# Attention scores cut into column tiles for the later tokens only, with two head pairs run last token first

## The chip, the cores and the metric

The kernel runs on one core of one Trainium2 chip. The metric is the device time of one execution in microseconds (us). The kernel before takes 520.03 us, the median of three runs (518.87 to 521.28).

## The reference

A linear attention with a decaying state feeds a two-layer network. For each of 4 batches and 8 heads (head size 48), over 768 tokens:

```
cur = einsum('bhd,bhe->bhde', u[None] * kt, vt)
y[:, :, t] = einsum('bhd,bhde->bhe', rt, state + cur)
state = wt[:, :, :, None] * state + einsum('bhd,bhe->bhde', kt, vt)
```

Then, with `x` the 3072 x 384 matrix of all heads' `y`: `h = x @ w_in` (2048 columns), `g = h` where `h > 0` and `exp(h) - 1` elsewhere, and the result is `g @ w_out` (384 columns).

## The kernel before, in words

The tokens are cut into 6 blocks of 128. A *unit* is one block of one batch: 24 units, numbered block by block, so units 8 to 23 are the third to the sixth block. In a unit the 8 heads are 4 *pairs* p; the two heads of a pair, q = 0 and 1, lie on partitions 0 to 47 and 64 to 111.

The work of a unit, with the short names that the order tables use:

- `es`, `gs` (DVE): running products of the decay; `kh` (DVE, line 404) multiplies k by them, `rh` (line 401) multiplies r.
- `s` (PE, line 458): the scores. For each pair and head one product of k (48 x 128 sources) with r (48 x 128 tokens), into two PSUM tiles `pa`, one for q = 0 and one for q = 1, each 128 sources x (4 pairs x 128 tokens). That is 8 products per unit in 32-bit floats; the trace has two matmul records for each such product (16 per unit).
- `sp` (ACT or POOL): writes the two tiles `am` with the diagonal term and zeros; `mk` (DVE, line 461, two per unit) copies into `am` the scores of later tokens (token after source), by the 0/1 mask `upper`.
- `v` (PE, line 488): y, in four column tiles of 32 output rows: from block 1 on 12 products of the state `st` with r, and always 16 products of v with `am`.
- `t` (PE, 466) transposes k, `kt` (ACT) copies it out, `u` (PE, 505) multiplies it with v, `up` (DVE, 513) adds that to the state; `sc` (DVE, 473) decays the state; `xh` (ACT) and `xl` (DVE, 498) split y into two parts for the network.

The network works on a block of all four batches (512 columns), in 16 slices of 128 hidden rows: `g1` (PE, line 248, nine matmuls), `r1`, `r2` (ACT), `stt` (DVE, 259), `gh` (ACT), `gl` (DVE, 270), `g2` (PE, line 281, nine matmuls). Blocks 0 and 1 run some slices in halves of 256 columns, so that there are 108 slices. The scores of the blocks ahead are worked off between the slices.

What sets the order: a table `ORDER` written out by hand gives each engine its list of tasks, and an engine works through its list in that order, waiting where an input or a buffer is not there. `ph`, the result of `g1`, has two buffers, so a `g1` waits for the `stt` of two slices before. The PSUM tiles `pa` are three, shared by `s`, `v`, `t`, `u` in turn. On PE the table reads, at the places that matter here, `t.8 s.9 v.8 g1.39 g2.36 g1.40 g2.37 u.8 v.9 s.10 g1.41`, and on DVE `mk.9.0 xl.8 up.8 rh.10 gl.38 stt.39 kh.11 mk.10.0 mk.10.1`. The table is the same in both kernels.

Of the kernel before, what the change touches and what calls it, by code (L numbers as in the profile page):

```python
# [8 lines left out]
F32 = mybir.dt.float32  # L9
F32R = mybir.dt.float32r  # L10
BF16 = mybir.dt.bfloat16
U32 = mybir.dt.uint32
# [4 lines left out]
ALU = mybir.AluOpType  # L17
AX = mybir.AxisListType

B, H, S, D = 4, 8, 768, 48  # L20
DM, DFF = 384, 2048
P = 128
C = 128
NC = S // C
NP = H // 2
# [5 lines left out]
CW = C + 1  # L31
# [1 line left out]
WKR = dict(w=(0, W1), k=(W1, W1 + K1), r=(W1 + K1, W1 + K1 + R1))  # L33
NU = NC * B
FH = (6, 6)
SIGN = "DVE"
WARM = 10


def _pieces():  # L40
# [274 lines left out]
def rwkv_elu_kernel(ctx, tc, wkr, rk, vp, u, uz, gkrw, gv, gu, w_in, w_out, out):  # L315
    nc = tc.nc
# [7 lines left out]
    cst = pool("cst", 1)  # L324
# [7 lines left out]
    tt, stt, act = nc.vector.tensor_tensor, nc.vector.scalar_tensor_tensor, nc.scalar.activation  # L332
# [6 lines left out]
    reset = cst.tile([R2, 2, NP, CW], F32, name="reset")  # L339
    lim = cst.tile([R2, 1], F32, name="lim")  # L340
    ident = cst.tile([P, P], F32, name="ident")
    upper = cst.tile([P, C], F32, name="upper")
    upper4 = upper.bitcast(U32).unsqueeze(1).broadcast_to([P, 4, C])
    ub = cst.tile([P, DM], F32, name="ub")
    ubd = cst.tile([R2, NP, 2], F32, name="ubd")
    tops = [cst.tile([P, 2, NK, P], U32, name=f"wt{n}") for n in range(SLOTS["wt"])]
# [4 lines left out]
    def constants():  # L351
        nc.scalar.preload_act_table_set("natural_log_exp_and_others")
        nc.vector.memset(reset, 2.0 ** -62)
        nc.vector.memset(reset[:, 0, :, C:CW], 1.0)
        nc.vector.memset(lim, -(2.0 ** 60))
        make_identity(nc, ident)
        nc.vector.memset(upper, 1.0)
        nc.gpsimd.affine_select(out=upper, in_=upper, pattern=[[1, C]], compare_op=ALU.is_gt,
                                fill=0.0, base=0, channel_multiplier=-1)
        for t in tops:  # L360
            nc.gpsimd.memset(t, 0)
        nc.gpsimd.memset(st, 0.0)
        nc.vector.memset(ones_c, 1.0)

    def warm():
        for _ in range(WARM):
            nc.tensor.matmul(first["accs"]()[0][:, 0:P], ident, ident, start=True, stop=True)
# [33 lines left out]
        tt(u_["r"], u_["r"], u_["eg"][:, 1, :, 0:C], ALU.mult)  # L401

    def k_hat(u_):
        tt(u_["k"], u_["k"], u_["eg"][:, 0, :, 1:CW], ALU.mult)

    def flag(u_):
        junk = at.tile([R2, 2 * NP * CW], BF16, tag="junk", name="junk", bufs=1)
# [43 lines left out]
    def score(u_):  # L451
        u_["pa"] = pa = [ps_a.tile([P, NP, C], F32, tag="pa", name="pa_s") for q in range(2)]
        for _ in range(FILL.get(("s", u_["i"]), 0) * (u_["i"] > 1)):
            nc.tensor.matmul(pa[0][:, 0], ident, ident, start=True, stop=True)
        for p in range(NP):
            for q in range(2):
                rs = slice(64 * q, 64 * q + D)
                nc.tensor.matmul(pa[q][:, p], u_["k"][rs, p, :], u_["r"][rs, p, :], start=True, stop=True)  # L458

    def mask(u_, q):  # L460
        nc.vector.copy_predicated(u_["am"][q], upper4, u_["pa"][q])  # L461

    def trans(u_):
        u_["pt"] = pt = ps_a.tile([P, NP, R2], F32, tag="pa", name="pa_t")
# [10 lines left out]
    def value(u_):  # L475
        c, b, v, am, rp = (u_[n] for n in ("c", "b", "v", "am", "r"))
        u_["py"] = py = ps_a.tile([P, NK, C], F32, tag="pa", name="pa_y")
        jobs = []
        if c > 0:
            for n in range(3 * NP):  # L480
                p, i = divmod(n, 3)
                jobs.append((n, st[:, b, p, 32 * i:32 * i + 32], rp[:, p, :]))
        for p, x in ROUNDS:
            jobs.append((3 * p + (0, 1, 1, 2)[x], v[:, P * p + 32 * x:P * p + 32 * x + 32], am[x // 2][:, p, :]))
        for n, (blk, l, r) in enumerate(jobs):
            k, j = divmod(blk, 4)
            same = [m for m, y in enumerate(jobs) if y[0] % 4 == j]
            nc.tensor.matmul(py[32 * j:32 * j + 32, k], l, r, start=(n == same[0]), stop=(n == same[-1]))  # L488
# [77 lines left out]
    for c in range(NC):  # L566
        fh = FH[c] if c < len(FH) else 0
        steps.append([(f, 0, N // 2) for f in range(fh)] + [(f, N // 2, N) for f in range(fh)] + [(f, 0, N) for f in range(fh, NF)])

    add(("const",), "POOL", constants)  # L570
    add(("warm",), "PE", warm, [("const",), ("es", 0)])
    add(("ubd",), "SP", lambda: load_u(True))
    add(("ub",), "SP", lambda: load_u(False))
    for u_ in units:
        i, c, b = u_["i"], u_["c"], u_["b"]
# [5 lines left out]
        add(("gs", i), "DVE", lambda u_=u_: g_scan(u_), [("es", i)])  # L581
        add(("rh", i), "DVE", lambda u_=u_: r_hat(u_), [("gs", i), ("ld_r", i)])
        add(("kh", i), "DVE", lambda u_=u_: k_hat(u_), [("es", i), ("ld_k", i)])
        if 0 < c:
            add(("pc", i), "ACT", lambda u_=u_: decay(u_), [("es", i)])
# [7 lines left out]
        else:  # L593
            e = DIAG[i]
# [6 lines left out]
        else:  # L601
            add(("sp", i), "POOL", lambda u_=u_: spread(u_), [("md", i)])
        add(("s", i), "PE", lambda u_=u_: score(u_), [("rh", i), ("kh", i), ("sp", i)])
        for q in range(2):
            add(("mk", i, q), "DVE", lambda u_=u_, q=q: mask(u_, q), [("s", i), ("sp", i)])
# [7 lines left out]
        if b:  # L613
            after.append(("v", i - 1))
        add(("v", i), "PE", lambda u_=u_: value(u_), after)
        add(("xh", i), "ACT", lambda u_=u_: x_high(u_), [("v", i)])
        add(("xl", i), "DVE", lambda u_=u_: x_low(u_), [("xh", i)])
# [11 lines left out]
    for c in range(NC):  # L629
        fns = mlp(nc, w_h, w_l, ps_acc, ps_h, ml, home, stg, out[:, c * N:(c + 1) * N], last=c == NC - 1)  # L630
        for f, lo, hi in steps[c]:
            s, n = dict(f=f, lo=lo, hi=hi), len(seq)
# [22 lines left out]
    for u_ in units:  # L655
        i, c = u_["i"], u_["c"]
# [13 lines left out]
    for f in range(NF):  # L670
        p = "raw0" if f % 3 == 0 or f == NF - 1 else "x1a" if f % 3 == 1 else "x1b"
# [10 lines left out]
    with tc.manual_schedule():  # L682
        for t in plan.order():
            k = t["key"]
# [128 lines left out]
```

## Time and profile before

| | |
|---|---|
| median of 3 runs | 520.03 us (518.87 to 521.28) |
| the profiled execution's own time | 521.82 us |
| its span, first to last instruction | 520.1 us |
| PE busy | 502.2 us (97%), 4065 matmul records |
| DVE / ACT / POOL busy | 331.2 / 276.1 / 66.0 us |
| mean granted TensorE clock | 0.995 |
| score matmuls (line 458) | 384 records in 24 units |

A row of a group reads: line, engine, operation, output and inputs, shapes, count, then busy time in us, the mean duration of one in ns, and the engine's idle time before them with what ended it. A row of the timeline reads: start, time from the first start to the last end, engine, line, operation, names, shapes, count. Matmuls overlap, so the count times the mean is far above the busy time; the end of a matmul record is modelled, and where it matters the starts are used: from the time of a timeline row one record's own duration is taken off, which leaves first start to last start.

### The profile page before, as it was taken

How to read it: one execution, taken by the hardware profiler on the slowest of the kernel's cores; microseconds unless marked ns; L12 is line 12 of the kernel's file. 1: busy time of each engine (PE TensorE's matmuls, PEld its weight loads, DVE VectorE, ACT ScalarE, POOL GpSimd, SP SyncE). 2: the span in 40 equal slices, each digit the busy share in tenths (PEclk: the TensorE clock that was granted, in tenths of full speed). 3: DMA queues.
4: the chain of work that ended last, by engine and by line, in shares of the span. 5: the costliest groups of instructions: out<-in, count | busy, mean ns of one | idle time of the engine just before them, and what ended most of it. 6: DMA issues, size and time to landing. Idle time of an engine off the chain costs nothing.

```text
span 520.1 us, 10015 instructions
## 1 busy us (share of the span) xinstructions
PE 502.2 (97%) x4065; PEld 423.7 (81%) x4065; DVE 331.2 (64%) x533; ACT 276.1 (53%) x558; POOL 66.0 (13%) x74
## 2 busy tenths in 40 slices
PE   4999999999999999999999999999999999999994
PEld 4788988889988888788888888888888788878884
DVE  7998889967677765756757476647474744333332
ACT  4979798757554434635444445325744524544441
POOL 2000000002131130701203021020220210000000
PEclk9989999999999999999999999999999999999999
DMA  7969463322224231322121336001440100000001
GB/s 223 325 218 281 140 204 113 92 68 88 78 77 134 86 100 39 124 87 88 56 70 38 94 105 194 2 1 38 143 127 8 69 1 1 26 36 3 0 2 64
DMA packets 26596, 47.35 MB, mean 91 GB/s; under 512 B 2736, under 2 KB 9008, under 8 KB 26544
## 3 DMA queue, kind: packets, MB, share of 16 engines
q1 hardware_dynamic: 26112, 45.86, 28.6%
q8 instruction: 34, 0.56, 0.4%
q10 hardware_dynamic: 432, 0.79, 0.4%
q14 instruction: 18, 0.15, 0.1%
HBM read 41.92 MB, written 4.72 MB: 90 GB/s over the span
## 4 chain that ended last, share of the span: by engine, by line
PE 86%; DVE 5%; ACT 2%; issue 1%; DMA 1%; SPq 0%; DVEq 0%; ACTq 0%
PE ph L248 36%; PE acc L281 36%; PE pa_y L488 6%; PE pa_s L458 4%; PE pa_u L505 2%; PE pa_t L466 1%; DVE m L259 1%; DMA r<-in_wkr_dram 1%; PE pa_d L428 1%; DVE gl L270 1%; DVE am L461 1%; ACT gh L266 0%; DVE r L401 0%; ACT m L256 0%; DVE xl L498 0%
## 5 line engine op out<-in xcount | busy, mean ns | idle before, releaser
L248 PE MATMUL ph<-xh,w_h 128*128 128x512 f32 (+1 forms) x324 | 122.1, 377 | 1.1 <-DVE m L259 1.0
L253 ACT ACTIVATE m<-ph 128x512 f32<-128x512 f32 (+1 forms) x108 | 59.3, 549 | 118.6 <-PE ph L248 78.6
L281 PE MATMUL acc<-gh,w_h 128*128 128x512 f32 (+1 forms) x325 | 120.7, 371 | 0.0
L248 PE MATMUL ph<-xl,w_h 128*128 128x512 f32 (+1 forms) x324 | 119.4, 369 | 1.2 <-DVE xl L498 1.2
L259 DVE SCALAR_TENSOR_TENSOR m<-m,ph 128x512 f32<-128x512 f32 (+1 forms) x108 | 67.0, 624 | 82.5 <-ACT m L256 82.2
L248 PE MATMUL ph<-xh,w_l 128*128 128x512 f32 (+1 forms) x324 | 119.5, 369 | 0.0
L281 PE MATMUL acc<-gl,w_h 128*128 128x512 f32 (+1 forms) x325 | 119.0, 366 | 0.3 <-DVE gl L270 0.3
L281 PE MATMUL acc<-gh,w_l 128*128 128x512 f32 (+1 forms) x325 | 118.7, 365 | 0.0
L270 DVE TENSOR_TENSOR gl<-m,gh 128x512 fp32r<-128x512 f32 (+1 forms) x108 | 68.9, 641 | 52.0 <-ACT gh L266 48.2
L266 ACT CAST gh<-m 128x512 fp32r<-128x512 f32 (+1 forms) x108 | 61.6, 571 | 70.3 <-PE acc L281 41.6
L248 PEld LDWEIGHTS ph<-xh,w_h 128*128 128x128 f32 x324 | 61.7, 191 | 13.3 <-DVE m L259 2.8
L248 PEld LDWEIGHTS ph<-xl,w_h 128*128 128x128 f32 x324 | 61.8, 191 | 10.5 <-DVE xl L498 1.4
L248 PEld LDWEIGHTS ph<-xh,w_l 128*128 128x128 f32 x324 | 61.8, 191 | 10.4 <-DVE w_l L552 0.2
L281 PEld LDWEIGHTS acc<-gl,w_h 128*128 128x128 f32 x325 | 61.3, 189 | 10.9 <-DVE gl L270 1.3
L281 PEld LDWEIGHTS acc<-gh,w_h 128*128 128x128 f32 x325 | 61.2, 188 | 10.8 <-issue 0.4
L281 PEld LDWEIGHTS acc<-gh,w_l 128*128 128x128 f32 x325 | 61.2, 188 | 9.8
L256 ACT ACTIVATE m<-m 128x512 f32<-128x512 f32 (+1 forms) x108 | 62.4, 583 | 1.5
L411 POOL TENSOR_TENSOR rk<-rk 128x384 f32<-128x384 f32 x16 | 17.8, 1115 | 221.9 <-DMA rk<-in_rk_dram 221.9
L461 DVE COPY_PREDICATED am<-upper,pa_s 128x512 f32<-128x512 uint32 x48 | 34.5, 744 | 16.9 <-PE pa_s L458 16.7
L446 POOL TENSOR_SCALAR_AFFINE_SELECT am<-md 128x512 f32<-128x512 f32 x32 | 27.7, 889 | 134.8 <-PE pa_y L488 101.0
L387 DVE TENSOR_TENSOR_SCAN eg<-w,reset 112x516 f32<-112x516 f32 x24 | 29.3, 1226 | 3.8 <-DMA w<-in_wkr_dram 3.2
L408 ACT ACTIVATE junk<-eg,lim 112x1032 bf16<-112x1032 f32 x24 | 27.7, 1155 | 7.3 <-DVE eg L397 7.2
(61 smaller groups left out, 471.0 us busy)
## 6 DMA issues: line engine op xcount, KB each, us to landing
v<-in_vp_dram SPq DMA_DIRECT2D x24, 256.0 KB, 4.0
rk<-in_rk_dram SPq DMA_DIRECT2D x16, 384.0 KB, 3.3
w<-in_wkr_dram SPq DMA_DIRECT2D x24, 226.2 KB, 3.7
k<-in_wkr_dram SPq DMA_DIRECT2D x24, 224.0 KB, 3.7
r<-in_wkr_dram SPq DMA_DIRECT2D x24, 224.0 KB, 4.1
out_dram<-o SPq DMA_DIRECT2D x15, 256.0 KB, 4.0
wrawx<-in_w_out_dram SPq DMA_DIRECT2D x10, 383.8 KB, 6.1
wrawx<-in_w_in_dram SPq DMA_DIRECT2D x10, 383.2 KB, 5.3
```

The source lines that it names most:

```text
L248: nc.tensor.matmul(ph[z:z + COLS], w[:, f, 0, k, z:z + COLS], x_[:, k, :], start=(k == n == 0), stop=(k == NK - 1 and n == 2))
L253: act(s["m"], s["ph"], AF.Relu, scale=-1.0)
L256: act(s["m"], s["m"], AF.Exp, scale=-1.0)
L259: stt_(s["m"], s["m"], -1.0, s["ph"], ALU.add, ALU.max)
L266: nc.scalar.copy(s["gh"], s["m"])
L270: nc.vector.tensor_tensor(s["gl"], s["m"], s["gh"].bitcast(F32), ALU.subtract)
L281: nc.tensor.matmul(a_[z:z + COLS], w[:, f, 1, m, z:z + COLS], g[:, s_], start=(f == n == 0 and lo == 0), stop=(f == NF - 1 and q == parts ...
L387: nc.vector.tensor_tensor_scan(out=flat(eg[:, 0]), data0=u_["w"][:, 1:W1][:, ::-1], data1=flat(reset[:, 0]), initial=0.0, op0=ALU.mult, op ...
L408: act(junk, u_["eg"].rearrange("d z p t -> d (z p t)"), AF.Relu, bias=lim, accum_out=flags[:, u_["i"]:u_["i"] + 1])
L446: nc.gpsimd.affine_select(out=am, in_=u_["md"][:, q::2].unsqueeze(2).broadcast_to([P, NP, C]), pattern=[[0, NP], [1, C]], compare_op=ALU.i ...
L461: nc.vector.copy_predicated(u_["am"][q], upper4, u_["pa"][q])
L488: nc.tensor.matmul(py[32 * j:32 * j + 32, k], l, r, start=(n == same[0]), stop=(n == same[-1]))
```

## The change

From unit 8 on (`TURN = 2`, so blocks 2 to 5), the scores of a pair and head are computed as four products of 32 sources each, in four column tiles, and each product takes only the tokens from its first source on: 128, 96, 64 and 32 tokens for tiles 0 to 3. For pairs 2 and 3 sources and tokens run last first (the host stores k, v and the r and k of the diagonal term reversed within a block for them, and r is read backwards), so that tile 3 has 128 tokens there and tile 0 has 32. `score_jobs` lists the 16 (pair, tile) steps, pairs in the order 0, 2, 1, 3, and each step is done for q = 0 and then q = 1. Pairs 0 and 2 share 160 columns of the PSUM tile, one filling what the other leaves; `windows` reads them back, 512 elements per partition as before, with a mask of two halves. `kh` is two instructions from unit 8 on, since the decay is read backwards for pairs 2 and 3, and `v` reads `am` backwards for these pairs. At the start `upper` is twice as wide and POOL makes it with two instructions.

```diff
+SC = 32
+TURN = 2
+PW = C + SC
+
+def score_jobs():
+    free, jobs = [0] * (P // SC), []
+    for p in (0, 2, 1, 3):
+        for t in sorted(range(P // SC), key=lambda t: (free[t], t)):
+            free[t] += C - SC * t if p < 2 else SC * t + SC
+            jobs.append((p, t))
+    return jobs
...
-    upper = cst.tile([P, C], F32, name="upper")
-    upper4 = upper.bitcast(U32).unsqueeze(1).broadcast_to([P, 4, C])
+    upper = cst.tile([P, 2, C], F32, name="upper")
+    uppers = upper.bitcast(U32).unsqueeze(2).broadcast_to([P, 2, 2, C])
+    upper4 = upper[:, 0].bitcast(U32).unsqueeze(1).broadcast_to([P, 4, C])
...
     def k_hat(u_):
-        tt(u_["k"], u_["k"], u_["eg"][:, 0, :, 1:CW], ALU.mult)
+        e = u_["eg"][:, 0, :, 1:CW]
+        if u_["c"] < TURN:
+            tt(u_["k"], u_["k"], e, ALU.mult)
+        else:
+            tt(u_["k"][:, 0:2], u_["k"][:, 0:2], e[:, 0:2], ALU.mult)
+            tt(u_["k"][:, 2:4], u_["k"][:, 2:4], e[:, 2:4, ::-1], ALU.mult)
...
-        for p in range(NP):
+        if u_["c"] < TURN:
+            for p in range(NP):
+                for q in range(2):
+                    rs = slice(64 * q, 64 * q + D)
+                    nc.tensor.matmul(pa[q][:, p], u_["k"][rs, p, :], u_["r"][rs, p, :], start=True, stop=True)
+            return
+        for p, t in score_jobs():
+            ts = slice(SC * t, SC * t + SC)
             for q in range(2):
-                rs = slice(64 * q, 64 * q + D)
-                nc.tensor.matmul(pa[q][:, p], u_["k"][rs, p, :], u_["r"][rs, p, :], start=True, stop=True)
+                rs, o = slice(64 * q, 64 * q + D), pa[q].rearrange("t p n -> t (p n)")
+                o = o[ts, PW * p + ts.stop:PW * p + PW] if p < 2 else o[ts, PW * (p - 2):PW * (p - 2) + ts.stop]
+                r = u_["r"][rs, p, ts.start:C] if p < 2 else u_["r"][rs, p, C - ts.stop:C][:, ::-1]
+                nc.tensor.matmul(o, u_["k"][rs, p, ts], r, start=True, stop=True)
...
     def mask(u_, q):
-        nc.vector.copy_predicated(u_["am"][q], upper4, u_["pa"][q])
+        am, pa = u_["am"][q], u_["pa"][q]
+        if u_["c"] < TURN:
+            nc.vector.copy_predicated(am, upper4, pa)
+        else:
+            pa = pa.rearrange("t p n -> t (p n)")[:, 0:2 * PW].rearrange("t (p n) -> t p n", p=2)
+            nc.vector.copy_predicated(am.rearrange("t (z p) n -> t z p n", z=2), uppers, windows(pa))
...
-            jobs.append((3 * p + (0, 1, 1, 2)[x], v[:, P * p + 32 * x:P * p + 32 * x + 32], am[x // 2][:, p, :]))
+            jobs.append((3 * p + (0, 1, 1, 2)[x], v[:, P * p + 32 * x:P * p + 32 * x + 32], am[x // 2][:, p, ::-1 if p > 1 and c >= TURN else 1]))
```

On PE, at unit 9's scores (between `t.8` and `v.8`; `pa_t` is the transposed k, `pa_s` the scores, `pa_y` the output y), the list reads before:

```order
L248 MATMUL ph<-xl,w_h 128x512
L248 MATMUL ph<-xh,w_l 128x512
L466 MATMUL pa_t<-ident,k 128x112 x4
L458 MATMUL pa_s<-r,k 128x128 x8
L488 MATMUL pa_y<-r,st 32x128 x12
L488 MATMUL pa_y<-am,v 32x128 x16
L248 MATMUL ph<-xh,w_h 128x512
```

Now, from the last of the four pairs on:

```order
L487 MATMUL pa_s<-r,k 32x128 x2
L487 MATMUL pa_s<-r,k 32x96 x2
L487 MATMUL pa_s<-r,k 32x64 x2
L487 MATMUL pa_s<-r,k 32x32 x2
L527 MATMUL pa_y<-r,st 32x128 x12
L527 MATMUL pa_y<-am,v 32x128 x16
L261 MATMUL ph<-xh,w_h 128x512
```

The four score rows stand four times in a row there, once for each pair: 32 products in the place of 8, and nothing else moved on PE.

On DVE, around `kh.10` (`k` is the product with the decay, `am` the masked scores, `eg` the decay products), before:

```order
L396 RECIPROCAL reset<-eg 112x4
L397 SCALAR_TENSOR_TENSOR eg<-w,reset 112x516
L404 TENSOR_TENSOR k<-k,eg 112x512
L461 COPY_PREDICATED am<-upper,pa_s 128x512
L259 SCALAR_TENSOR_TENSOR m<-m,ph 128x512
```

Now:

```order
L411 RECIPROCAL reset<-eg 112x4
L412 SCALAR_TENSOR_TENSOR eg<-w,reset 112x516
L423 TENSOR_TENSOR k<-k,eg 112x256
L424 TENSOR_TENSOR k<-k,eg 112x256
L500 COPY_PREDICATED am<-upper,pa_s 128x512
L272 SCALAR_TENSOR_TENSOR m<-m,ph 128x512
```

One instruction became two of half the size, in each of the 16 units from unit 8 on; the masks keep their place, number and size.

More of the change, by code (lines that the diff above doesn't have):

```diff
@@ L35 @@
 FH = (6, 6)
-SIGN = "DVE"
 WARM = 10
+SC = 32
[8 more added lines that the diff above has]
+    return jobs
 def _pieces():
@@ L357, in constants @@
         nc.vector.memset(upper, 1.0)
-        nc.gpsimd.affine_select(out=upper, in_=upper, pattern=[[1, C]], compare_op=ALU.is_gt,
-                                fill=0.0, base=0, channel_multiplier=-1)
+        for z in range(2):
+            nc.gpsimd.affine_select(out=upper[:, z], in_=upper[:, z], pattern=[[1 - 2 * z, C]], compare_op=ALU.is_gt,
+                                    fill=0.0, base=0, channel_multiplier=2 * z - 1)
         for t in tops:
@@ L454, in score, with windows @@
             nc.tensor.matmul(pa[0][:, 0], ident, ident, start=True, stop=True)
-        for p in range(NP):
-            for q in range(2):
-                rs = slice(64 * q, 64 * q + D)
-                nc.tensor.matmul(pa[q][:, p], u_["k"][rs, p, :], u_["r"][rs, p, :], start=True, stop=True)
-    def mask(u_, q):
-        nc.vector.copy_predicated(u_["am"][q], upper4, u_["pa"][q])
+        if u_["c"] < TURN:
[6 more added lines that the diff above has]
+            ts = slice(SC * t, SC * t + SC)
+            for q in range(2):
+                rs, o = slice(64 * q, 64 * q + D), pa[q].rearrange("t p n -> t (p n)")
+                o = o[ts, PW * p + ts.stop:PW * p + PW] if p < 2 else o[ts, PW * (p - 2):PW * (p - 2) + ts.stop]
+                r = u_["r"][rs, p, ts.start:C] if p < 2 else u_["r"][rs, p, C - ts.stop:C][:, ::-1]
+                nc.tensor.matmul(o, u_["k"][rs, p, ts], r, start=True, stop=True)
+    def windows(pa):
+        x = pa[:, :, SC:PW].unsqueeze(1).broadcast_to([P, 2, 2, C])
+        return bass.AP(x.tensor, x.offset, [x.ap[0], [-SC, 2], *x.ap[2:]])
+    def mask(u_, q):
+        am, pa = u_["am"][q], u_["pa"][q]
[4 more added lines that the diff above has]
+            nc.vector.copy_predicated(am.rearrange("t (z p) n -> t z p n", z=2), uppers, windows(pa))
     def trans(u_):
@@ L781 @@
     k = pairs(inputs["k"])
+    k[TURN:, :, :, 2:] = k[TURN:, :, :, 2:, ::-1]
     r = pairs(inputs["r"])
@@ L784 @@
     tok = lambda x: x.reshape(B, H, NC, C, D).transpose(2, 0, 3, 1, 4).reshape(NC, B, C, 1, DM)
-    rk = np.concatenate([tok(inputs[n]) for n in "rk"], axis=3)
-    vp = tok(inputs["v"]).reshape(NC, B, C, NP, 2, D)
+    turn = lambda x: np.concatenate([x[..., 0:DM // 2], np.concatenate([x[0:TURN], x[TURN:, :, ::-1]])[..., DM // 2:]], axis=-1)
+    rk = np.concatenate([turn(tok(inputs[n])) for n in "rk"], axis=3)
+    vp = turn(tok(inputs["v"])).reshape(NC, B, C, NP, 2, D)
     vp = np.concatenate([vp[..., 0, :], np.zeros((NC, B, C, NP, 32), np.float32), vp[..., 1, :]], axis=-1).reshape(NC, B, C, NP * P)
```

## The prediction

> **What bounds the kernel now.** I read the page's shares first, then the chain that ended last, then PE's waits from the third block on.
>
> ```profile
> PE 502.2 (97%) x4065; PEld 423.7 (81%) x4065; DVE 331.2 (64%) x533; ACT 276.1 (53%) x558; POOL 66.0 (13%) x74
> PE 86%; DVE 5%; ACT 2%; issue 1%; DMA 1%; SPq 0%; DVEq 0%; ACTq 0%
> PE ph L248 <- DVE m L259: 1.0, 1, 1.0
> PE acc L281 <- DVE gl L270: 0.3, 1, 0.3
> ```
>
> PE is the bound: the chain is 86% PE, and between 140 and 440 us, where all the changed scores lie, it waited for other engines twice, 1.3 us in all. What a stage takes on PE there goes to the end, unless the next instruction waits for something else. So the question is what the scores take, and the timeline of PE at unit 9 shows it.
>
> ```profile
> 163.98 0.39 PE L248 MATMUL ph<-xh,w_l 128*128 128x512 f32 x1
> 164.21 0.55 PE L466 MATMUL pa_t<-ident,k 112*128 112x112 f32 x4
> 164.68 1.16 PE L458 MATMUL pa_s<-r,k 48*128 48x128 f32 x16
> 165.78 0.86 PE L488 MATMUL pa_y<-r,st 112*32 112x128 f32 x24
> 166.45 1.06 PE L488 MATMUL pa_y<-am,v 128*32 128x128 f32 x32
> 167.44 0.50 PE L248 MATMUL ph<-xh,w_h 128*128 128x512 f32 x1
> ```
>
> Eight score products are 16 records, two halves each. One record lasts 0.272 us (row below), so the last starts 1.16 - 0.27 = 0.89 us after the first.
>
> ```profile
> L458 PE MATMUL pa_s<-r,k x384: 272/272/579, 11.9 to 431.3; 48*128 48x128 f32 x192
> L367 PE MATMUL acc<-ident x20: 275/275/377, 20.4 to 22.6; 128*128 128x128 f32 x20
> L488 PE MATMUL pa_y<-r,st x480: 270/273/297, 91.7 to 433.8; 112*32 112x128 f32 x160
> 165.78 0.32 PE L488 MATMUL pa_y<-r,st 112*32 112x128 f32 x4
> ```
>
> On the whole array such a record takes 2.2 / 19 = 0.116 us of its own (line 367, 20 records from 20.4 to 22.6). The scores' 16 in 0.89 us are twice as dense: two heads run at once, in two row halves. The values are four times as dense: the 32 of line 488 start within 1.06 - 0.27 = 0.79 us, eight rounds of four, (0.79 - 0.02) / 7 = 0.110 us a round. The last row shows the first four of such a group: 0.32 us from first start to last end with 0.297 us each, so four column tiles start within 0.023 us, 0.0077 apart. The layout that the change asks for, two row halves times four column tiles, stands nowhere in this trace; its two factors do.
>
> **The change, part by part: the scores.** A unit's stream now lasts 0.89 + 0.11 (the last round) = 1.00 us. Afterwards there are 32 products, 64 records, eight to each of the eight tiles. What one takes by its columns comes from the 128 columns above and from line 505, 48 columns in two column tiles:
>
> ```profile
> 175.83 0.56 PE L505 MATMUL pa_u<-v,kt 128*48 128x48 f32 x16
> L505 PE MATMUL pa_u<-v,kt x320: 208/208/243, 23.8 to 401.2; 128*48 128x48 f32 x160
> ```
>
> Sixteen in eight rounds of two: (0.56 - 0.208) / 7 = 0.050 us a round, somewhat high, since the first one holds a weight load. A line through both points has 0.75 ns a column and 14 ns beside it: 0.086 us for 96 columns, 0.062 for 64, 0.038 for 32. Tile 0 then has 4 x 0.110 + 4 x 0.038 = 0.592 us, tile 1 has 4 x 0.086 + 4 x 0.062 = 0.592; the reversal of two pairs makes all tiles equal. Before the first record comes a load of 32 columns, 0.297 - 0.272 = 0.025 us, and the eighth tile starts 7 x 0.0077 = 0.054 us late. Sum 0.67 us, saving **0.33 us a unit**. With 45 ns for 48 columns, if that first round is taken as long, a tile has 0.565 and the saving is 0.36; this is the better end. The change of layout ahead of the scores and behind them stays: 165.78 - (164.68 + 0.89 + 0.11) = 0.10 us behind them now.
>
> What the sum needs is that 64 records can be issued in 0.67 us, one per 10.5 ns; at one per 15.6 ns nothing is left. Three paces stand in the trace. Four tiles started 7.7 ns apart; that is a short burst. A longer one comes at unit 2, where PE's sequencer had been held and the queue had run empty:
>
> ```profile
> L488 PEldq EVENT_SEMAPHORE  x1: 1127/1127/1127, 37.5 to 37.5; - x1
> L488 PEld LDWEIGHTS pa_y<-am,v x8: 106/106/109, 38.6 to 38.7; 128*32 128x32 f32 x8
> 38.63 0.19 PEld L488 LDWEIGHTS pa_y<-am,v 128*32 128x32 f32 x8 [0.20 <-PE pa_s L458]
> ```
>
> Released at 37.5 + 1.1 = 38.6, it had eight weight loads of eight records going by 38.63 + 0.19 - 0.109 = 38.71, at most 13 ns a record with the wake-up in it. The slowest pace is line 505's, 0.35 / 15 = 23.5 ns over 16 records, but there the two tiles are full, which bounds it by itself. I take the first, since in both other rows the tiles or the wake-up explain the time, and keep the others as rivals.
>
> [...]
>
> **Where the saving does not arrive.** 15 of the 16 units pass it on. At unit 10 the chain goes round PE:
>
> ```profile
> 175.90 0.52 PE pa_u L505 x16
> ...
> 176.44 0.35 DVE st L513
> ...
> 177.19 0.69 DVE r L401
> 177.88 0.60 DVE gl L270
> ...
> 178.51 0.70 DVE m L259
> 179.21 0.04 issue
> 179.26 0.50 PE ph L248
> 177.99 1.16 PE L458 MATMUL pa_s<-r,k 48*128 48x128 f32 x16
> ```
>
> From `u.8` it runs over `up.8`, `rh.10`, `gl.38` and `stt.39` on DVE to `g1.41`; the scores of unit 10 lie beside it and would have let `g1.41` go at 177.99 + 0.89 + 0.20 = 179.08, so 0.18 us before it went. Nothing is gained there. Elsewhere the distance from a unit's scores to its masks and on to its values is kept, as all of them come earlier.
>
> **DVE and the start.** `kh` in two halves:
>
> ```profile
> L404 DVE TENSOR_TENSOR k<-k,eg x24: 665/684/1505, 10.2 to 422.2; 112x512 f32<-112x512 f32 x24
> 145.61 0.43 DVE L270 TENSOR_TENSOR gl<-m,gh 128x256 fp32r<-128x256 f32 x1 [1.44 <-ACT gh L266]
> L461 DVE COPY_PREDICATED am<-upper,pa_s 128x512 f32<-128x512 uint32 x32 | 23.3, 744 | 15.6 <-PE pa_s L458 15.6
> sum 376.00, PE 372.16 PEld 306.02 DVE 213.56 ACT 172.32 POOL 58.28; mean PE 62.03 PEld 51.00 DVE 35.59 ACT 28.72 POOL 9.71
> L411 POOL TENSOR_TENSOR rk<-rk 128x384 f32<-128x384 f32 x16 | 17.8, 1115 | 221.9 <-DMA rk<-in_rk_dram 221.9
> ```
>
> Two of 0.43 for one of 0.68 is 0.18 us a unit, 2.9 us of DVE in all; from 140 us to 516 DVE is busy 214 of 376 us, and before the masks it waits 15.6 us for the scores themselves. That covers it: 0; without the cover, 2.9. At unit 10 the chain holds no `kh` (`kh.10` is ahead of `mk.9.1`, which waits for PE; `kh.11` comes after `stt.39`). The masks read as many elements, 744 ns. The second `affine_select` on POOL at the start lies in its 221.9 us of idle time: 0. The reversed reads on PE have no row; bounds are nothing and half speed (below), and I take nothing, because DVE's scan with reversed reads takes no longer than the one without:
>
> ```profile
> L397 DVE TENSOR_TENSOR_SCAN eg<-w,reset 112x516 f32<-112x516 f32 x14 | 17.5, 1249 | 0.5
> L387 DVE TENSOR_TENSOR_SCAN eg<-w,reset 112x516 f32<-112x516 f32 x14 | 17.1, 1224 | 2.2 <-DMA w<-in_wkr_dram 1.6 <-ACT junk L408 0.5
> ```
>
> **Sum.** 15 x 0.33 = 5.0 us. The profiled execution's own 521.82 us (span 520.1 and 1.7 around it, which the change does not touch) becomes 516.8; it lies 1.8 above the median of the runs, so from 520.03 the forecast is **515.0 us**.
>
> **Rivals.**
> - *Issue is the bound (slower).* If 64 records go at line 505's 23.5 ns, a unit takes 64 x 0.0235 + 0.05 = 1.55 us, 0.55 more; 16 x 0.55, less the 0.18 of unit 10, is +8.6: 528.6. It decides from 15.6 ns on. For it: no row shows more than eight records faster. Against it: the 7.7 and 13 ns. [...] 7%.
> - *Issue at 13 ns:* 64 x 0.013 + 0.04 = 0.87, saving 0.13 x 15 = 2.0: 518.0. 9%.
> - *Only four tiles at once,* as in line 488: the mean record is 0.592 / 8 = 0.074 us, 16 rounds 1.18 + 0.05 = 1.23 us; 16 x 0.23 - 0.18 = +3.5: 523.5. Against it: row halves and column tiles each work alone. 5%.
> - *Reversed reads at half speed:* half of the scores' 0.592 is 0.30; in the values pairs 2 and 3 have 16 records, four to a tile, 4 x 0.110 = 0.44. 16 x (0.74 - 0.33) = +6.6: 526.6. 5%.
> - [...] 2%.
>
> **Numbers.** The forecast has 72%; its own range, 513.0 to 517.2, takes in the 0.36 (5.4 us) and a shift of the median of some 1.2 us, as the three runs show. The whole range, 512.8 to 519.0, adds the 13 ns case and leaves out the last four, 19% and a little. A measurement tells 0.5%, 2.6 us, from no change. Faster by that (under 517.4): most of the forecast and a part of the 13 ns case, 0.73. Within it: the rest of these and a part of the four-tile case, 0.11. Slower: 0.16.
>
> **What would show it.** The score row of unit 9 should read 64 records, first to last start 0.55 to 0.65 us, and eight starts within 0.06 us; four by four would be the third rival, an even spacing of 13 or 23 ns the first two. The values should keep 0.79 us from first to last start (else the reversed reads cost), masks 744 ns, and PE's waits from 140 to 440 us should grow by unit 10's 0.4 us or so only. The forecast is wrong if the scores shrink as said and PE then waits for DVE elsewhere.

## The result, and the profile after

The changed kernel takes **516.93 us**, the median of 8 runs (515.82 to 517.61), against 519.48 us for the kernel before (median of 8 now, 518.87 to 521.28). The ratio is 0.9946, with a 95% interval of 0.9931 to 0.9961: 2.55 us less, where 5.0 were forecast. The middle of the ratio lies just beyond the prediction's bound of 0.5%, but its interval reaches back over it; the saving is about half of what was expected.

The first lines of the page after, and PE's waits between 140 and 440 us:

```profile
PE 498.4 (97%) x4833; PEld 419.7 (82%) x4833; DVE 333.2 (65%) x549; ACT 276.0 (54%) x558; POOL 65.5 (13%) x75
PE 86%; DVE 6%; ACT 2%; issue 1%; ACTq 0%
PE ph L261 <- DVE m L272: 1.4, 2, 1.1
```

PE is still the bound and still waits hardly at all (1.3 us before, 1.4 now), so the missing half isn't a new wait for another engine. It should lie in the scores. PE's timeline in the first of the changed units, unit 9 and the last unit (start, time from first start to last end, count at the end):

```profile
142.77 1.00 PE L487 MATMUL pa_s<-r,k 48*32 48x128 f32 x64
...
162.35 1.00 PE L487 MATMUL pa_s<-r,k 48*32 48x128 f32 x64
163.28 0.86 PE L527 MATMUL pa_y<-r,st 112*32 112x128 f32 x24
163.96 1.06 PE L527 MATMUL pa_y<-am,v 128*32 128x128 f32 x32
...
425.91 1.00 PE L487 MATMUL pa_s<-r,k 48*32 48x128 f32 x64
```

From the scores' first start to the next group's first start it is now 163.28 - 162.35 = 0.93 us; before it was 165.78 - 164.68 = 1.10 (1.091 by the starts to the nanosecond, 0.931 now, in each of the 16 units but unit 10). So a unit saves 0.16 us, not 0.33, and 15 x 0.16 = 2.4 us is nearly the whole gain of 2.55. By the starts, the last record begins 0.731 us after the first, where 0.55 to 0.65 was expected. How the 64 records of unit 9 get going is seen in windows that all begin with the first of them (columns: window, its length, PE busy and, in brackets, how many records have begun by its end; granted clock last but two):

```profile
162.35:162.40 0.05, 0.05 (x8) 1.00 0.00 0
162.35:162.63 0.28, 0.28 (x32) 1.00 0.00 0
162.35:162.67 0.32, 0.32 (x32) 1.00 0.00 0
162.35:162.77 0.42, 0.42 (x33) 1.00 0.00 0
162.35:162.92 0.57, 0.57 (x43) 1.00 0.00 0
162.35:163.09 0.74, 0.74 (x64) 1.00 0.00 0
```

Eight start within 0.05 us and 32 within 0.28, which is a pace of 64 in 0.56 and all that the forecast needs. Then, from 0.28 to 0.42 us, **one** record starts. After that they come again, but the time is gone. The clock is 1.00 throughout, and PE's program holds no semaphore wait inside the block. What the first and the 33rd to 41st records do, from the trace (1 and 2 in the order of the program, the others in the order of their starts; start after the first one in ns, duration in ns, columns; the ends, and so the durations, are modelled):

```
record     start   duration
 1           0       293    128 columns, first half of product 1
 2         133       269    128 columns, second half of product 1
33         320       267    128 columns
34         429       267    128 columns
35..       437, 454, 470, 487, 504, 520, 537
```

Record 33 starts 27 ns after record 1 has ended (293), the next one 27 ns after record 2 has ended (133 + 269 = 402). From the 35th on the starts are 16.6 ns apart, one for a product of four instructions (two weight loads and two records).

**Theory W.** By 277 ns 32 records have started, each with a weight load of its own, and the next record starts at 320. Read as a rule: PE takes in at most 64 instructions ahead, 32 weight loads and 32 records (the 33rd load starts at 272 ns, after the first load's end at 101). Inside that window a record may start as soon as its tile is free, also ahead of earlier ones (the seventh product's second half starts at 92 ns, the first product's at 133). But a place comes free in program order: instruction n + 64 enters only when instruction n, and all before it, have ended (the 27 ns behind the ends of records 1 and 2); then they come in at 4.15 ns each (16.6 / 4). The order matters: both records of the seventh product (32 columns) had ended by 40 + 213 = 253 and 92 + 193 = 285 ns, and if any ended record freed a place, record 34 would have come soon after 285 + 27 = 312 ns and not at 429. A replay follows the block record by record under W's rule and adds up the times. With the 27 ns and 4.15 ns of the rows above, and a tile kept for 109, 82, 56 and 29 ns by a record of 128, 96, 64 and 32 columns (starts on one tile in this unit), it gives 0.73 us from first to last start (measured 0.731); without the limit of 64 it gives 0.56 us and a stream of 0.62, near the forecast's 0.67. As its numbers come from this very block, the agreement here is no test of it; the experiments are. **Theory I** is what the forecast named as a rival: PE issues so many small records at a pace of its own, 0.731 / 63 = 11.6 ns each.

### The profile page after: what moved, and what is told of

Its sections match the earlier page's. It is cut to its first block, busy times and chain, and to the rows that moved or that the text cites. A ratio compares the mean times of both kernels' runs of the same rounds, so it can differ in the third digit from the quotient of the medians.

```text
span 514.1 us, 11587 instructions
## 1 busy us (share of the span) xinstructions
PE 498.4 (97%) x4833; PEld 419.7 (82%) x4833; DVE 333.2 (65%) x549; ACT 276.0 (54%) x558; POOL 65.5 (13%) x75
## 4 chain that ended last, share of the span: by engine, by line
PE 86%; DVE 6%; ACT 2%; issue 1%; ACTq 0%
PE acc L294 37%; PE ph L261 36%; PE pa_y L527 6%; PE pa_s L487 3%; PE pa_u L544 2%; PE pa_t L505 1%; PE pa_s L479 1%; DVE am L497 1%; DVE m L272 1%; PE pa_d L448 1%; DVE gl L283 1%; DVE w_l L591 1%; DVE wg L584 0%; DVE eg L412 0%; ACT gh L279 0%
## 5 line engine op out<-in xcount | busy, mean ns | idle before, releaser
L466 POOL TENSOR_SCALAR_AFFINE_SELECT am<-md 128x512 f32<-128x512 f32 x32 | 26.4, 850 | 132.0 <-PE pa_y L527 97.2
L500 DVE COPY_PREDICATED am<-upper,pa_s 128x512 f32<-128x512 uint32 x32 | 23.2, 742 | 15.0 <-PE pa_s L487 14.9
```

Source lines behind the costliest of these rows:

```text
L466: nc.gpsimd.affine_select(out=am, in_=u_["md"][:, q::2].unsqueeze(2).broadcast_to([P, NP, C]), pattern=[[0, NP], [1, C]], compare_op=ALU.i ...
L500: nc.vector.copy_predicated(am.rearrange("t (z p) n -> t z p n", z=2), uppers, windows(pa))
```

## The experiments

Each changes the changed kernel, in units 8 to 23 only. The replay's numbers were not fitted again.

### The order of the products

```diff
 def score_jobs():
-    free, jobs = [0] * (P // SC), []
-    for p in (0, 2, 1, 3):
...
+    return [(0, 3), (2, 0), (0, 2), (1, 1), (3, 3), (0, 0), (3, 2), (0, 1), (2, 3),
+            (2, 2), (1, 0), (2, 1), (3, 1), (1, 2), (1, 3), (3, 0)]
```

> The same 32 score products of a unit in another order, so that no long product is among those whose end is waited for late. Theory W (a window of 64 instructions on PE, 32 weight loads and 32 records, released in program order: instruction n+64 enters only when instruction n and all before it have ended): a replay of the block with this window gives 0.65 us from the first to the last record's start, against 0.73 in the changed kernel, and the stream ends 0.16 us earlier: 15 x 0.16 = 2.4 us, 514.5 us. Theory I (PE issues these small records at 11.6 ns each, whatever their order): 0.73 us again, 516.9 us.

The other way round, the longest first (in place of the same lines):

```diff
+    return [(0, 0), (1, 0), (2, 3), (3, 3), (0, 1), (1, 1), (2, 2), (3, 2), (0, 2),
+            (1, 2), (2, 1), (3, 1), (0, 3), (1, 3), (2, 0), (3, 0)]
```

> The same 32 products, all of 128 columns first, then all of 96, 64 and 32. Theory W: the first 32 records are the longest, in two tile rows at a time, and hold the window longest: 0.94 us from the first to the last start, and the stream ends 0.12 us later than in the changed kernel: 16 x 0.12 less unit 10's part, some +1.8 us on the whole. Theory I (11.6 ns a record, whatever the order): 0.73 us, no change.

Unit 9's scores in the first kernel, windows from their first start, and PE's waits between 140 and 440 us; then scores and windows of the second kernel:

```profile
163.33 0.84 PE L480 MATMUL pa_s<-r,k 48*32 48x32 f32 x64
...
163.33:163.61 0.28, 0.28 (x30) 1.00 0.00 0
163.33:163.75 0.42, 0.42 (x41) 1.00 0.00 0
...
PE ph L254 <- DVE m L265: 1.8, 2, 1.4
PE acc L287 <- DVE gl L276: 0.4, 1, 0.4
```

```profile
164.21 1.13 PE L480 MATMUL pa_s<-r,k 48*32 48x128 f32 x64
...
164.21:164.61 0.40, 0.40 (x32) 1.00 0.00 0
164.21:164.85 0.64, 0.64 (x37) 1.00 0.00 0
```

From first to last start it is 0.652 us (0.84 less the last record's 0.19) and 0.936; W said 0.65 and 0.94, I 0.73 for both. The same 64 records of the same sizes take 0.28 us more or less by their order alone, so no fixed pace is the limit: theory I falls. At 0.42 us the good order has 41 records going where the changed kernel has 33; the bad one has 37 at 0.64. The first takes 515.35 us (ratio to before 0.9922, 0.9897 to 0.9947), the second 519.73 in its one run, where some 518.7 was expected. The first was expected at 514.5: PE waits 2.2 us for DVE in it where the changed kernel waits 1.4, and these 0.8 us are what W's sum, which knows only the scores, leaves out.

### How many records fit

Two pairs instead of four:

```diff
-    for p in (0, 2, 1, 3):
+    for p in (0, 2):
...
-        return bass.AP(x.tensor, x.offset, [x.ap[0], [-SC, 2], *x.ap[2:]])
+        return bass.AP(x.tensor, x.offset, [x.ap[0], [-SC, 2], [0, 2], *x.ap[3:]])
```

> From the third block on only the scores of head pairs 0 and 2 are computed (32 records in place of 64; the masks copy them for pairs 1 and 3 too, so half of the scores is left out and everything else stays). Theory W: 32 records and their 32 weight loads fit the window, nothing waits for a release: 0.28 us from first to last start, as the tiles' own work gives it, and the kernel is 15 x 0.45 = 6.8 us below the changed one, 510. Theory I: 31 x 11.6 ns = 0.36 us, 15 x 0.37 = 5.5 us, 511.4.

Three pairs (0, 2, 1), with the same second line:

> From the third block on only the scores of pairs 0, 2 and 1 (48 records a unit; the masks copy those of pairs 0 and 2 for the rest, so a quarter of the scores is left out). Theory W: records 33 to 48 wait for the release of the oldest ones: 0.596 us from first to last start. Theory I (11.6 ns a record): 47 x 0.0116 = 0.545 us. With no limit but the tiles' own work it would be 0.418.

All products with 32 columns, the mask reading the same 32 for all (its lines left out here):

```diff
-                nc.tensor.matmul(o, u_["k"][rs, p, ts], r, start=True, stop=True)
+                nc.tensor.matmul(pa[q].rearrange("t p n -> t (p n)")[ts, SC * p:SC * p + SC], u_["k"][rs, p, ts], r[:, 0:SC], start=True, stop=True)
```

> All 32 products of a unit with 32 columns each (64 records; the scores of the other columns are left out, the masks copy the same 32 columns for all). The tiles have little to stream, 8 x 0.029 = 0.23 us each. Theory W: the second 32 records still wait until the first ones have ended, some 0.2 us after their start, and then come at 8.3 ns a record: 0.569 us from first to last start. Theory I (11.6 ns a record): 0.73 us as in the changed kernel. With no limit but 4.15 ns an instruction: 0.43 us.

Unit 9 with two pairs, and PE's waits between 140 and 440 us there; with three pairs; with short products, and its windows:

```profile
162.46 0.51 PE L487 MATMUL pa_s<-r,k 48*32 48x128 f32 x32
...
PE ph L261 <- DVE m L272: 2.2, 2, 1.5
PE acc L294 <- DVE gl L283: 0.4, 1, 0.4
PE pa_y L527 <- ACT kt L509: 0.4, 2, 0.2
PE pa_u L544 <- ACT kt L509: 0.2, 1, 0.2
```

```profile
162.68 0.84 PE L487 MATMUL pa_s<-r,k 48*32 48x128 f32 x48
```

```profile
162.42 0.76 PE L487 MATMUL pa_s<-r,k 48*32 48x32 f32 x64
...
162.42:162.59 0.17, 0.17 (x32) 1.00 0.00 0
162.42:162.66 0.24, 0.24 (x32) 1.00 0.00 0
162.42:162.70 0.28, 0.28 (x34) 1.00 0.00 0
```

First to last start: 0.278 us with two pairs (W 0.28, I 0.36), 0.589 with three (W 0.596, I 0.545, no limit 0.418), 0.565 with short products (W 0.569, I 0.73, no limit 0.43). The short products show the window best: 32 records start in 0.17 us, then none for 0.07 us although every tile is nearly empty. By the trace record 33 starts at 242 ns and record 34 at 274, each 28 ns after the (modelled) end of the oldest and of the second oldest record, 214 and 246. The kernel with short products took 515.82 us, that with three pairs 516.37, one run each; single runs of one kernel lie up to 4.2 us apart here (516.58 to 520.78 in the experiment with one multiplication below), so these two times tell little. With two pairs the time was 512.58 us, where W's sum said 510: the scores had 0.45 us less, but PE then waited 3.2 us in all instead of 1.4, among others for `kt` on ACT, which a longer score block had covered. So W tells these blocks to some 7 ns; it doesn't tell the whole, once other waits come to light.

### A tile of 64 sources

```diff
-SC = 32
+SC = 64
```

> Column tiles of 64 sources in place of 32: 16 products and 32 records a unit, each again for its later tokens only, everything else as in the changed kernel. Theory W: 32 records with their loads are exactly one window, so nothing waits for a release, though a tile has more to stream; the replay gives 0.663 us from first to last start and a stream that ends 0.11 us before that of the changed kernel: 15 x 0.11 = 1.65 us, 515.3 us. Against W: were it something else that holds the second half of a block back, the last 16 of these 32 records would come late as well, 0.7 us or more, and the time would be 516.9 or above.

```profile
163.88 0.90 PE L487 MATMUL pa_s<-r,k 48*64 48x128 f32 x32
164.71 0.86 PE L527 MATMUL pa_y<-r,st 112*32 112x128 f32 x24
```

First to last start is 0.667 us (W 0.663), and from scores to values it is 0.83 us against 0.93. So half as many products, with 16% more to stream in a tile (0.688 against 0.592 us by the prediction's line), make the shorter block here. The time is 516.54 us, median of 5 (514.91 to 518.1), with a ratio of 0.9916 (0.9886 to 0.9946); it lies on W's side (515.3 / 519.5 = 0.992), but the interval reaches the changed kernel's 0.9946, so the whole time doesn't tell the two apart.

### What the rest of the change costs

The scores as whole products of 128 columns again, the rest of the change left in place:

```diff
-        for p, t in score_jobs():
...
+        for p in range(NP):
+            for q in range(2):
+                rs = slice(64 * q, 64 * q + D)
+                nc.tensor.matmul(pa[q][:, p], u_["k"][rs, p, :], u_["r"][rs, p, ::-1 if p > 1 else 1], start=True, stop=True)
```

> The scores as whole products of 128 columns again (16 records, all tokens), everything else as in the changed kernel: last token first for two pairs, reversed reads in scores and values, the multiplication by the decay in two halves, the second mask. If these cost nothing, as the prediction has it, the time is the kernel's before, 519.5 us, with 0.89 us from first to last score and 0.79 in the values. If the reversed reads or the halves cost the 2.4 us that the forecast misses, it is 522.

```profile
163.88 1.16 PE L484 MATMUL pa_s<-r,k 48*128 48x128 f32 x16
164.97 0.86 PE L523 MATMUL pa_y<-r,st 112*32 112x128 f32 x24
165.65 1.06 PE L523 MATMUL pa_y<-am,v 128*32 128x128 f32 x32
```

Scores and values last as long as before (0.890 and 0.786 us from first to last start): the reversed reads cost nothing. The time is 521.16 us, a ratio of 1.0022 (1.0000 to 1.0043): some 1.1 us more, with nothing just inside the interval. That lies between the two times expected, 519.5 and 522, so the rest of the change may cost something, though not in the scores or the values. Where a cost could lie is shown by the one longer wait of PE, near 219 us, in the four kernels, in this order: before, this one, the changed kernel, and the next experiment:

```profile
220.56 0.50 PE L248 MATMUL ph<-xh,w_h 128*128 128x512 f32 x1 [1.00 <-DVE m L259]
```

```profile
220.36 0.50 PE L261 MATMUL ph<-xh,w_h 128*128 128x512 f32 x1 [1.60 <-DVE m L272]
```

```profile
218.10 0.50 PE L261 MATMUL ph<-xh,w_h 128*128 128x512 f32 x1 [1.10 <-DVE m L272]
```

```profile
218.31 0.50 PE L261 MATMUL ph<-xh,w_h 128*128 128x512 f32 x1 [1.02 <-DVE m L272]
```

The chain on DVE that this wait hangs on holds two units' `kh`, and 1.00 became 1.60 with the halves here (1.10 in the changed kernel). That gave a theory D: the halves cost where this chain runs. The next experiment has one multiplication again:

```diff
-        e = u_["eg"][:, 0, :, 1:CW]
-        if u_["c"] < TURN:
-            tt(u_["k"], u_["k"], e, ALU.mult)
-        else:
-            tt(u_["k"][:, 0:2], u_["k"][:, 0:2], e[:, 0:2], ALU.mult)
-            tt(u_["k"][:, 2:4], u_["k"][:, 2:4], e[:, 2:4, ::-1], ALU.mult)
+        tt(u_["k"], u_["k"], u_["eg"][:, 0, :, 1:CW], ALU.mult)
```

> The multiplication of k by the decay in one instruction for all four pairs, all else as in the changed kernel; for pairs 2 and 3 the decay is then applied in the wrong order of tokens, which is the part of the computation that changes. Theory D (the two halves cost 0.18 us of DVE a unit and this is hidden but in one place, near 218 us, where PE waits for a chain on DVE that holds two such products): PE's one wait for m shrinks from 1.1 to 0.7 us, some 0.4 us on the whole, 516.5 us. Rival (the cover is complete, as the prediction has it): the wait stays at 1.1, 516.9 us.

It takes 517.37 us (ratio 0.9950, 0.9927 to 0.9973), no less than the changed kernel, and the wait is 1.02 us, not 0.7: theory D falls as a fixed price. Why, the groups of DVE between 205 and 222 us show, of the changed kernel and of this one:

```profile
L424 DVE TENSOR_TENSOR k<-k,eg 112x256 f32<-112x256 f32 x2 | 2.1, 1046 | 0.0
L423 DVE TENSOR_TENSOR k<-k,eg 112x256 f32<-112x256 f32 x2 | 1.8, 885 | 0.0
L416 DVE TENSOR_TENSOR r<-r,eg 112x512 f32<-112x512 f32 x2 | 1.4, 681 | 0.0
L512 DVE TENSOR_TENSOR st<-st,pc 112x384 f32<-112x384 f32 x1 | 0.5, 547 | 0.0
```

```profile
L419 DVE TENSOR_TENSOR k<-k,eg 112x512 f32<-112x512 f32 x2 | 2.8, 1375 | 0.0
L416 DVE TENSOR_TENSOR r<-r,eg 112x512 f32<-112x512 f32 x2 | 1.8, 900 | 0.0
L507 DVE TENSOR_TENSOR st<-st,pc 112x384 f32<-112x384 f32 x1 | 1.0, 984 | 0.0
```

In the changed kernel half a `kh` takes 0.89 to 1.05 us in the mean against the prediction's 0.43 (0.42 in most other units), while `r` and `st` have their usual 0.68 and 0.55. With one multiplication a whole `kh` takes 1.4 against 0.68, and `st` and the first `r` are long as well (0.98 and 1.12 us). What `kh` loses in one kernel, `r` and `st` lose in the other (5.8 us in sum in the changed kernel, 5.6 here). The long ones all begin while POOL works on `rk` and `am`, until 214.75 us in the changed kernel and until 215.76 here; the `st` and `r` that begin after that have their usual times. In the kernel before POOL works on them until 219.65 us: `kh` (1.17 us in the mean), `st` (1.37) and the first `r` (1.11) begin ahead of that and are long, and the `r` that begins at 220.43 has 0.69. So these rows of DVE are long where POOL is busy beside them; but `gl` between them keeps its 0.68 us and no run took POOL's work away, so that POOL is the cause is not shown.

### The best order by theory W

```diff
+    return [(2, 0, 0), (0, 3, 1), (2, 0, 1), (3, 0, 0), (2, 1, 0), (1, 2, 0), (0, 2, 1), (3, 0, 1),
...
-        for p, t in score_jobs():
+        for p, t, q in score_jobs():
...
-            for q in range(2):
+            if True:
```

> The 32 products of a unit in an order that was searched with the replay of theory W, the two row halves apart. Theory W: 0.61 us from first to last start and a stream that ends at 0.66 us, so 0.34 us less a unit than before the change; 15 units pass it on: 5.1 us, a ratio of 0.990 to the kernel before, some 514.4 us. A part of it may be lost where a DVE chain already holds PE (near 177 and 218 us). Theory I (11.6 ns a record): 0.73 us and the time of the changed kernel, 516.9 us, a ratio of 0.995.

```profile
163.42 0.83 PE L480 MATMUL pa_s<-r,k 48*32 48x32 f32 x64
164.18 0.86 PE L520 MATMUL pa_y<-r,st 112*32 112x128 f32 x24
...
163.42:163.69 0.28, 0.28 (x33) 1.00 0.00 0
163.42:163.83 0.42, 0.42 (x43) 1.00 0.00 0
```

The stall is gone: 43 records by 0.42 us, no two starts in a row more than 27 ns apart (109 in the changed kernel), 0.622 from first to last start (W 0.61), and 0.76 us from scores to values: 0.33 less than before, which is the saving of the forecast. The time is **515.23 us** (median of 6, 513.71 to 516.78), the ratio to before 0.9908 (0.9886 to 0.9930), some 4.8 us. W's sum gave 514.4; PE waits 2.2 us for DVE here too, 0.8 more than in the changed kernel. Of the kernels that compute all scores it has the lowest time, with the same products as the changed one, and its interval lies just below that kernel's; the order of 16 steps (515.35) can't be told from it.

## Why the prediction was right, and where it was not

- **The sign and the mechanism held.** The gain is shorter scores on PE, 15 units' worth: 15 x 0.16 = 2.4 of the 2.55 us measured. The eight tiles work at once (eight starts in 0.046 us; forecast 0.054) and the first half of the products runs at the forecast's pace, 32 records in 0.277 us. Rival three (four tiles at a time) is refused by the eight starts. Nor do the records of unit 9 start in the order of the program, as two starts show: the seventh product, of 32 columns, starts its second half 92 ns after the first start, ahead of the first product's second half at 133.
- **The term that was mis-sized** is the unit's 0.67 us, and the step behind it: "What the sum needs is that 64 records can be issued in 0.67 us ... I take the first". The paces that it weighed came from bursts of 4 and 8 records, 8 and 16 instructions. The block has 128, and the first stall came after 32 records and their loads, half of it. The measured stream is 0.84 us (0.93 less the change of layout, 0.09), of which W (0.62 without the limit) puts 0.22 down to the wait for the oldest records to end and the refilling.
- **The limit that counted** has no term in the forecast. In unit 9 there is no stall up to 32 records with their loads (0.277 us) and a stall from the 33rd on (0.320 us, the 34th at 0.429); with two pairs, 32 records in all, the block takes the 0.278 us of the tiles' own work. The starts fit places that come free in program order (27 ns after the ends of the first and the second record), while records on different tiles pass each other (92 ns ahead of 133).
- **The rival "issue at 13 ns"** came close in time (0.87 us a unit, 518.0 us), though not in kind: there is no even spacing, and the order of the products moves the block from 0.62 to 0.94 us. Its place was taken by a mechanism that none of the prediction's rows shows. 516.93 lies in the forecast's own range by luck: its base was 520.03, from which the measured saving gives 517.48, beyond that range's 517.2. The median of the kernel before came out 0.55 us lower, a shift that the range allowed for without knowing its side.
- **Unit 10** passes nothing on, as said. In the row below PE waits for `stt.39` there, and from its last score to `g1.41` it is 0.532 us where it was 0.377: 0.155 of the 0.16 saved are lost.

```profile
175.54 1.00 PE L487 MATMUL pa_s<-r,k 48*32 48x128 f32 x64
176.81 0.50 PE L261 MATMUL ph<-xh,w_h 128*128 128x512 f32 x1 [0.26 <-DVE m L272]
```

- **Reversed reads, 0:** shown by the whole products (0.890 and 0.786 us). **Masks:** 742 ns in the row below, 744 before.

```profile
L500 DVE COPY_PREDICATED am<-upper,pa_s 128x512 f32<-128x512 uint32 x32 | 23.2, 742 | 15.0 <-PE pa_s L487 14.9
```

- **`kh` in halves, 0:** not refuted by the time, since one multiplication brought nothing (517.37 us). But the cover is not complete, as the prediction had it: near 219 us PE waits for DVE already in the kernel before, that wait (1.00 us) was quoted and not followed up, and with the halves it was 1.10 to 1.60 us (1.02 with one multiplication again).
- **The two profiled executions** differ by 6.0 us of span, far more than the medians. Some 2.2 of it lies ahead of unit 4's scores, where the change touches only the making of the mask:

```profile
74.56 1.16 PE L458 MATMUL pa_s<-r,k 48*128 48x128 f32 x16
```

```profile
72.39 1.16 PE L479 MATMUL pa_s<-r,k 48*128 48x128 f32 x16
```

In the two kernels of the first experiment, with the same work at the start, they stand at 73.5 and 74.1 us. A gain of half a per cent is therefore read from the stage that changed and from medians, not from two spans.

## What to carry to other kernels

When a matmul is cut into many small ones, count the records and their weight loads: up to 32 records with their loads the tiles alone set the time here (0.278 us for 32); beyond, the oldest unfinished ones did (0.731 us for 64, where the replay without that limit gives 0.56). Then put the products in such an order that the early places come free soon (no long chain on one tile at the front, short products at the very end, as in the two better orders), or cut into fewer, larger tiles: 16 products of 64 sources took 0.83 us a unit, 32 of 32 took 0.93 in the changed kernel's order and 0.76 in the best. The pace of bursts of 4 and 8 records said nothing here about a block of 64.

## What the runs showed of the hardware

The rule that fits is theory W: PE runs ahead by 64 instructions (in the changed kernel's unit 9, 32 records with their loads had started by 0.277 us and the 33rd record came at 0.320), released in program order (the 33rd and the 34th start 27 ns after the ends of the first and the second). With its numbers from the changed kernel's unit 9 it gives the first-to-last start in eight kernels (us; the first row is the one that the numbers come from, the others stood on record before their run):

| kernel | records | by W | measured |
|---|---|---|---|
| the changed kernel | 64 | 0.73 | 0.731 |
| order of 16 steps | 64 | 0.65 | 0.652 |
| longest first | 64 | 0.94 | 0.936 |
| two pairs | 32 | 0.28 | 0.278 |
| tiles of 64 sources | 32 | 0.663 | 0.667 |
| three pairs | 48 | 0.596 | 0.589 |
| short products | 64 | 0.569 | 0.565 |
| order of 32 steps | 64 | 0.61 | 0.622 |

Every record here has a weight load of its own (64 of each in unit 9), so whether the window counts 64 instructions or 32 records stays open. Inside it, in the changed kernel's unit 9, eight tiles of 48 rows and 32 columns work at once, their first starts 6.7 ns apart (eight in 0.046 us), and records of different tiles pass each other (a second half at 92 ns ahead of an earlier one at 133).
